# Weights in column halves and a new order of loads and engines in an attention and channel-mix kernel

## The chip, the cores and the metric

The kernel runs on one core of a Trainium2 chip. The metric is the device time in microseconds of one execution; the time before is the median of six runs.

## What is computed

```python
def _attn_ref(q, k, v):                      # q, k, v: 8 x 8 x 576 x 64, float32
    q_s = softmax of q over its last axis (64)
    k_s = softmax of k over the sequence (576)
    kv = np.einsum('bhsd,bhse->bhde', k_s, v)
    return np.einsum('bhsd,bhde->bhse', q_s, kv)

def _moe_ref(x, mu_k, mu_r, w_k, w_v, w_r):  # x: 8 x 576 x 512, heads side by side
    x_prev = x shifted by one row of the sequence, zero first
    xk = mu_k * x + (1.0 - mu_k) * x_prev
    xr = mu_r * x + (1.0 - mu_r) * x_prev
    k = np.maximum(xk @ w_k, 0.0)            # w_k: 512 x 1024
    v = k * k @ w_v                          # w_v: 1024 x 512
    r = 1.0 / (1.0 + np.exp(-(xr @ w_r)))    # w_r: 512 x 512
    return (r * v).astype(np.float32)
```

(The two softmaxes are written as words here.)

## The kernel before

Batches b are 0 to 7, and the eight heads of a batch are taken in two groups g of four. For each (b, g) the kernel loads q, k and v (line 308), takes exponentials on ACT (445), sums and scales the rows of q on DVE (458 to 466), transposes q on TensorE (498), sums kv (475), copies the transposed q (503), and multiplies it with kv (511). For batches 0 and 1 (ON_PE) the mix with mu is folded into the weights wp (555), so that TensorE writes the mixed xk and xr, which are evicted by ACT or DVE (568). For the others x is copied (605, 608), and DVE forms differences, scales and sums (617 to 627). xk and xr are rings of four batches in bfloat16.

The channel mix runs over units of 512 columns of that ring (the last of each half is 256). In a unit the eight products with columns of wk come first (712), each four matmuls over the 512 channels, then relu on ACT (697) and the square on DVE (701). Then for each 128 rows come the product with wr (745), its tanh (750), the product with wv in two halves of four matmuls (755), the gate on DVE (761) and the store (772). The first two units (early) take wk in two passes, four products on the first half of the channels, which group g = 0 makes, then on the second half. Four PSUM banks mm_a to mm_d serve all these products, and two double banks att_a and att_b serve the attention.

Weights are loaded by POOL's queue, which converts float32 to bfloat16: wk in two loads by channel pairs (wk0 for g = 0, wk1 for g = 1), wr in one, wv in two (wv0, wv1). The inputs of batch 0 are loaded by SP's and ACT's queues; those of batch 1 in halves by POOL, named by q, k or v, the batch, the group and a or b: q10a is the first half of q of batch 1, group 0. LOADS gives the order of POOL's queue up to the end of batch 1. The first load of POOL waits for the load first[GATE].

A planner in the kernel (class Plan) decides the order of every engine before anything runs. Each operation has an engine, an occupation, a latency, operations it waits for and buffers it takes and frees. set_due works backward: an operation is due ahead of what needs it by its latency, HOP and SPARE, and by its own early, which for the mixing operations is EARLY[2b + g] less EARLY_R when it makes xr. The products of the channel mix have due times from a running clock that starts at MAIN and grows by PACE times the product's time. order then plays the program through: the engine whose operation can start first takes it, and among operations that can start within LOOK of now the one due first. Loads take size/DMA_RATE each in one line, and a load of POOL counts as landed some time later. The emitted order is final: every engine runs its queue in order on the chip. ALONE says up to which (b, g) a pending product of q with kv is put in a block of its own, ahead of the next transposition, and after which it is joined with that. [...]

Of the kernel before, what the change touches and what calls it, by code (L numbers as in the profile page):

```python
# [18 lines left out]
LATE = 1e6  # L19
SPARE = 0.142  # L20
LOOK = {"PE": 0.017, "ACT": 0.686, "DVE": 0.274, "POOL": 0.03, "SP": 0.03}
EARLY = (-0.88, 2.53, 7.27, 7.81, 6.48, 1.05, 4.91, 4.86, 2.31, 3.67, 7.48, 5.23, -5.83,
         4.63, 1.92, 1.86)
EARLY_R = -0.92
MAIN = 17.0
PACE = 1.05
DMA_RATE = 404.0
# [6 lines left out]
ORDER = (0, 1, 2)  # L34
LOADS = ("wk0", "q10b", "wk1", "v10a", "q10a", "wr", "k10a", "wv0", "mu", "v10b", "k10b",
         "wv1", "k11b", "q11b", "q11a", "k11a", "v11a", "v11b")
GATE = 7
FILL = 0
FILL_AT = 1
FILL_END = 15.0  # L40
ON_PE = (0, 1)
CASTS = (("POOL", "POOL"), ("ACT", "DVE"), ("ACT", "ACT"))
QCOPY = ("ACT", "ACT", "DVE")
WIDE = "ACT"
ALONE = 8
EVAC = ((("ACT", "DVE"), ("ACT", "DVE")), (("DVE", "ACT"), ("ACT", "ACT")))
# [25 lines left out]
class Plan:  # L72
# [60 lines left out]
    def order(self):  # L133
# [15 lines left out]
        while left:  # L149
# [59 lines left out]
def kernel(  # L209
# [12 lines left out]
    nc = tc.nc  # L222
# [49 lines left out]
    def bank(slot):  # L272
        return ps[slot.pool][slot.index][:]
# [103 lines left out]
    rows_done = plan.add("PE", 0.86, 0.98, -501, emit_mu_rows, [rows_load, consts], [rows_slot])  # L377
    wide = plan.add(WIDE, 0.48 if WIDE == "ACT" else 0.6, 0.6 if WIDE == "ACT" else 0.7, 0, emit_mu_wide, [rows_done], [], [rows_slot])
    mu_split = [plan.add("POOL", 0.5, 0.6, -2 + m, lambda m=m: emit_mu_rest(m), [wide])
                for m in range(2)]  # L380

    def filler(slot):
        for _ in range(2):
            nc.tensor.matmul(bank(slot)[:, 0:128], lhsT=ident[:], rhs=ident[:], start=True,
                             stop=True)
# [23 lines left out]
    def emit_wv(h):  # L409
        n = FT // 2  # L410
        ap = bass.AP(tensor=moe_w_v.tensor, offset=moe_w_v.offset + h * n * C,
                     ap=[[FT * C, 128], [C, n], [1, C]])
        return nc.gpsimd.dma_start(out=wv_bf[:, h * n:(h + 1) * n, :], in_=ap)
# [262 lines left out]
    for _ in range(FILL):  # L676
        slot = Slot("mm")
        plan.add("PE", 0.12, 0.25, 2 * LATE, lambda slot=slot: filler(slot), [warmed[0]], [slot],
                 [slot])
# [5 lines left out]
    def unit(half, c0, n):  # L685
# [24 lines left out]
        def k_part(kf, fc, cts):  # L710
            for ct in cts:
                nc.tensor.matmul(bank(kf)[:, 0:n],  # L712
                                 lhsT=wk_bf[:, ct, fc::FT],
                                 rhs=xs[0][:, ct, c0:c0 + n],
                                 start=(ct == 0), stop=(ct == CT - 1))
# [134 lines left out]
```

## Time and profile before

| | |
|---|---|
| median of 6 runs | 203.84 us (202.52 to 204.48) |
| the profiled execution | 202.52 us |
| its span | 200.8 us |
| TensorE matmuls busy | 183.5 us (91%) |
| TensorE weight loads busy | 103.9 us (52%) |
| VectorE busy | 162.2 us (81%) |
| ScalarE busy | 137.3 us (68%) |
| GpSimd busy | 40.5 us (20%) |
| bytes moved | 40.72 MB, 203 GB/s on average |

Times within the profile are from the start of the span, which is shorter than the run's time by what lies around the program. Busy shares are averages over the span: which engine sets the time is read stage by stage, from the slices and from the chain that ended last. Moved bytes count a converting load by what it writes, half of what it reads.

### The profile page before, as it was taken

What the parts mean: (1) busy time and instruction counts of PE and PEld (TensorE: products, weight loads), DVE (VectorE), ACT (ScalarE), POOL (GpSimd) and SP (SyncE); (2) the same over time, 40 slices, a digit from 0 to 9 for tenths busy, and PEclk for the clock granted to TensorE, in tenths of its full rate; (3) what the DMA queues carried; (4) which work ended last, traced back from release to release, by engine and by line L of the source; (5) the groups of instructions that cost most, each with busy time, mean ns of one, the idle gap of its engine ahead of it and who ended that gap; (6) DMA issues with size and microseconds to landing.
All of it is one profiled execution on the core that took longest, in us unless ns stands there. A gap on an engine that the chain in (4) does not pass through costs nothing.

```text
span 200.8 us, 5308 instructions
## 1 busy us (share of the span) xinstructions
PE 183.5 (91%) x2146; PEld 103.9 (52%) x2171; DVE 162.2 (81%) x348; ACT 137.3 (68%) x212; POOL 40.5 (20%) x65
## 2 busy tenths in 40 slices
PE   2557899899999999999999999999999999999992
PEld 0234554446444654564476564456446554654761
DVE  2697755897999999999989999999999879732531
ACT  5583797699899789867499788945744652552440
POOL 1592447643153212501230000000000000000000
PEclk9999999999999999999999999999999999999999
DMA  6999999999999998994986130342026112402514
GB/s 191 388 247 276 239 288 405 389 401 412 386 401 402 405 370 256 295 363 141 320 264 208 31 76 3 69 96 49 3 54 136 24 44 64 105 0 52 118 42 105
DMA packets 15249, 40.72 MB, mean 203 GB/s; under 512 B 2285, under 2 KB 3065, under 8 KB 15225
## 3 DMA queue, kind: packets, MB, share of 16 engines
q0 software_dynamic: 7568, 27.40, 41.2%
q1 hardware_dynamic: 7208, 12.26, 21.0%
q10 hardware_dynamic: 448, 0.72, 1.2%
q8 instruction: 17, 0.28, 0.6%
q14 instruction: 8, 0.06, 0.1%
HBM read 33.56 MB, written 9.44 MB: 214 GB/s over the span
## 4 chain that ended last, share of the span: by engine, by line
PE 85%; DVE 6%; DMA 4%; issue 2%; ACT 1%; DVEq 0%; ACTq 0%
PE mm_b L755 10%; PE mm_d L712 9%; PE mm_c L712 8%; PE mm_c L755 7%; PE mm_d L755 7%; PE mm_a L755 7%; PE mm_b L712 7%; PE mm_a L712 5%; PE mm_c L745 4%; PE mm_a L745 4%; PE mm_d L745 3%; PE mm_b L745 3%; PE att_a L511 3%; PE att_b L511 3%; DMA raw_d<-in_q_dram 3%; PE att_b L498 2%
## 5 line engine op out<-in xcount | busy, mean ns | idle before, releaser
L712 PEld LDWEIGHTS <-wk_bf 128*128 128x128 bf16 x320 | 43.5, 144 | 20.8 <-issue 2.2
L712 PE MATMUL mm_d<-xk,wk_bf 128*128 128x512 bf16 (+1 forms) x94 | 23.9, 367 | 0.1
L755 PEld LDWEIGHTS <-k_b 128*128 128x128 bf16 x152 | 14.3, 98 | 15.3 <-issue 0.5
L745 PEld LDWEIGHTS <-xr 128*128 128x128 bf16 x144 | 13.9, 98 | 15.9 <-issue 0.2
L755 PEld LDWEIGHTS <-k_a 128*128 128x128 bf16 x144 | 13.4, 98 | 15.7 <-issue 0.9
L712 PE MATMUL mm_c<-xk,wk_bf 128*128 128x512 bf16 (+1 forms) x80 | 19.9, 357 | 0.6 <-issue 0.6
L712 PE MATMUL mm_b<-xk,wk_bf 128*128 128x512 bf16 (+1 forms) x75 | 18.9, 363 | 0.1
L712 PE MATMUL mm_a<-xk,wk_bf 128*128 128x512 bf16 (+1 forms) x62 | 15.3, 358 | 0.2
L755 PE MATMUL mm_b<-wv_bf,k_b 128*128 128x512 bf16 (+1 forms) x54 | 13.3, 363 | 0.2 <-issue 0.2
L745 PE MATMUL mm_c<-wr_bf,xr 128*128 128x512 bf16 x43 | 11.2, 379 | 0.1
L745 PE MATMUL mm_a<-wr_bf,xr 128*128 128x512 bf16 x39 | 10.2, 379 | 0.1
L755 PE MATMUL mm_c<-wv_bf,k_a 128*128 128x512 bf16 x39 | 10.1, 379 | 0.2 <-issue 0.2
L755 PE MATMUL mm_b<-wv_bf,k_a 128*128 128x512 bf16 x38 | 9.8, 379 | 0.2 <-issue 0.2
L755 PE MATMUL mm_a<-wv_bf,k_a 128*128 128x512 bf16 x30 | 8.1, 380 | 0.1
L755 PE MATMUL mm_d<-wv_bf,k_a 128*128 128x512 bf16 x32 | 8.2, 380 | 0.0
L755 PE MATMUL mm_d<-wv_bf,k_b 128*128 128x512 bf16 x32 | 8.2, 379 | 0.0
L745 PE MATMUL mm_d<-wr_bf,xr 128*128 128x512 bf16 x31 | 8.2, 379 | 0.1
L750 ACT ACTIVATE th_a<-mm_c 128x512 f32<-128x512 f32 x10 | 6.0, 603 | 3.1 <-PE mm_c L745 3.1
L755 PE MATMUL mm_a<-wv_bf,k_b 128*128 128x512 bf16 x29 | 7.6, 379 | 0.5 <-issue 0.5
L750 ACT ACTIVATE th_b<-mm_a 128x512 f32<-128x512 f32 x7 | 4.2, 604 | 4.5 <-PE mm_a L745 2.3
L755 PE MATMUL mm_c<-wv_bf,k_b 128*128 128x512 bf16 (+1 forms) x31 | 7.1, 352 | 0.2 <-issue 0.2
L745 PE MATMUL mm_b<-wr_bf,xr 128*128 128x512 bf16 x26 | 7.1, 379 | 0.1
(268 smaller groups left out, 415.4 us busy)
## 6 DMA issues: line engine op xcount, KB each, us to landing
out_dram<-ot_a SPq DMA_DIRECT2D x24, 128.0 KB, 4.2
out_dram<-ot_b SPq DMA_DIRECT2D x24, 128.0 KB, 3.4
out_dram<-ot_c SPq DMA_DIRECT2D x22, 128.0 KB, 2.4
raw_a<-in_q_dram POOLq DMA_DIRECT2D x3, 576.0 KB, 7.3
raw_c<-in_v_dram POOLq DMA_DIRECT2D x3, 576.0 KB, 8.0
raw_b<-in_k_dram POOLq DMA_DIRECT2D x2, 576.0 KB, 9.9
raw_d<-in_q_dram POOLq DMA_DIRECT2D x2, 576.0 KB, 10.6
raw_e<-in_k_dram POOLq DMA_DIRECT2D x2, 576.0 KB, 9.4
```

Source lines behind the costliest of these rows:

```text
L498: nc.tensor.transpose(out=transposed()[64 * u:64 * u + 64, hf, 64 * j:64 * j + 64], in_=qss[qs.index][r, j, 64 * u:64 * u + 64], identity= ...
L511: nc.tensor.matmul(bank(xp)[64 * hf:64 * hf + 64, u, at + c:at + e], lhsT=w[r, hf, :], rhs=qts[qt.index][r, hf, src:src + e - c], start=(n ...
L712: nc.tensor.matmul(bank(kf)[:, 0:n], lhsT=wk_bf[:, ct, fc::FT], rhs=xs[0][:, ct, c0:c0 + n], start=(ct == 0), stop=(ct == CT - 1))
L745: nc.tensor.matmul(bank(rps), lhsT=xs[1][:, ct, c:c + 128], rhs=wr_bf[:, ct // 2 + 2 * (ct % 2), :], start=(ct == 0), stop=(ct == CT - 1))
L750: nc.scalar.activation(out=ths[th.index][:], in_=bank(rps), func=ACT.Tanh, scale=0.5)
L755: nc.tensor.matmul(bank(vps)[:, 0:w], lhsT=k2s[k2.index][:, ft, 128 * m:128 * m + 128], rhs=wv_bf[:, ft, e:e + w], start=(ft == 0), stop=( ...
```

## The change

wk0, the part of wk for the first group's channels, is loaded in two column halves, wk0a and wk0b (columns 0 to 511 and 512 to 1023). The product fc used every eighth column from fc; it now uses every fourth column of one half, so that products 0 to 3 need wk0a and products 4 to 7 need wk0b. The rows of wv are loaded in the matching order. LOADS is another order: q10a comes first, then all of wk, and both parts of wv come later. The planner's constants SPARE, LOOK, EARLY, EARLY_R, MAIN, PACE, FILL_END and ALONE, its sizes of the weight loads and its allowance for a POOL load to land are others, so the order of all engines is another. The filler has another form, and the number of fillers stays 0; the choice of the engine for the wide copy of mu is written in another way, and stays ACT.

```diff
-SPARE = 0.142
-LOOK = {"PE": 0.017, "ACT": 0.686, "DVE": 0.274, "POOL": 0.03, "SP": 0.03}
-EARLY = (-0.88, 2.53, 7.27, 7.81, 6.48, 1.05, 4.91, 4.86, 2.31, 3.67, 7.48, 5.23, -5.83,
-         4.63, 1.92, 1.86)
-EARLY_R = -0.92
-MAIN = 17.0
-PACE = 1.05
+SPARE = 0.367
+LOOK = {"PE": 0.014, "ACT": 0.49, "DVE": 0.274, "POOL": 0.03, "SP": 0.03}
+EARLY = (-4.56, 2.11, 8.25, 13.06, 6.4, 0.7, -0.55, -0.78, 2.62, 0.78, 6.17, 8.08, -3.7,
+         4.17, 15.59, 5.15)
+EARLY_R = 3.13
+MAIN = 14.0
+PACE = 1.2
...
-LOADS = ("wk0", "q10b", "wk1", "v10a", "q10a", "wr", "k10a", "wv0", "mu", "v10b", "k10b",
-         "wv1", "k11b", "q11b", "q11a", "k11a", "v11a", "v11b")
+LOADS = ("q10a", "wk0a", "wk0b", "wk1", "k10a", "q10b", "wr", "mu", "v10b", "v10a", "k10b",
+         "wv0", "q11b", "wv1", "q11a", "k11b", "k11a", "v11a", "v11b")
...
-FILL_END = 15.0
+FILL_END = 14.0
...
-ALONE = 8
+ALONE = 6
...
                 if op.engine == "POOL":
-                    op.end += 1.4 if op.size > 1000 else 0.6
+                    op.end += 1.0 if op.size > 600 else 0.8
...
-    def emit_wk(g):
-        ap = bass.AP(tensor=moe_w_k.tensor, offset=moe_w_k.offset + g * 128 * F,
-                     ap=[[F, 128], [256 * F, 2], [1, F]])
-        return nc.gpsimd.dma_start(out=wk_bf[:, 2 * g:2 * g + 2, :], in_=ap)
+    def emit_wk(g, c, e):
+        ap = bass.AP(tensor=moe_w_k.tensor, offset=moe_w_k.offset + g * 128 * F + c,
+                     ap=[[F, 128], [256 * F, 2], [1, e - c]])
+        return nc.gpsimd.dma_start(out=wk_bf[:, 2 * g:2 * g + 2, c:e], in_=ap)
...
-    wk_done, wv_done = [], []
-    for g in range(2):
-        wk_done.append(plan.add("POOL", 0.8, 0.8, LOADS.index(f"wk{g}"), lambda g=g: emit_wk(g), gate,
-                                size=1140.0))
-    wr_done = plan.add("POOL", 0.8, 0.8, LOADS.index("wr"), emit_wr, gate, size=1140.0)
+    wk_done, wv_done = {}, []
+    for name in LOADS:
+        if name.startswith("wk"):
+            g = int(name[2])
+            c, e = {"": (0, F), "a": (0, F // 2), "b": (F // 2, F)}[name[3:]]
+            o = plan.add("POOL", 0.8, 0.8, LOADS.index(name),
+                         lambda g=g, c=c, e=e: emit_wk(g, c, e), gate, size=1250.0 * (e - c) / F)
+            for h in range(2):
+                if c <= h * F // 2 < e:
+                    wk_done[g, h] = o
+    wr_done = plan.add("POOL", 0.8, 0.8, LOADS.index("wr"), emit_wr, gate, size=1200.0)
...
     def emit_wv(h):
         n = FT // 2
-        ap = bass.AP(tensor=moe_w_v.tensor, offset=moe_w_v.offset + h * n * C,
-                     ap=[[FT * C, 128], [C, n], [1, C]])
+        ap = bass.AP(tensor=moe_w_v.tensor, offset=moe_w_v.offset + h * n * 128 * C,
+                     ap=[[n * C, 128], [C, n], [1, C]])
         return nc.gpsimd.dma_start(out=wv_bf[:, h * n:(h + 1) * n, :], in_=ap)
 
     for h in range(2):
         wv_done.append(plan.add("POOL", 0.8, 0.8, LOADS.index(f"wv{h}"), lambda h=h: emit_wv(h), gate,
-                                size=1140.0))
+                                size=1200.0))
...
                 nc.tensor.matmul(bank(kf)[:, 0:n],
-                                 lhsT=wk_bf[:, ct, fc::FT],
+                                 lhsT=wk_bf[:, ct, F // 2 * (fc // 4) + fc % 4:F // 2 * (fc // 4 + 1):4],
                                  rhs=xs[0][:, ct, c0:c0 + n],
                                  start=(ct == 0), stop=(ct == CT - 1))
...
-                        + [wk_done[h] for h in gs] + [mms_[i]],
+                        + [wk_done[h, fc // 4] for h in gs] + [mms_[i]],
```

More of the change, by code (lines that the diff above doesn't have):

```diff
@@ L377 @@
     rows_done = plan.add("PE", 0.86, 0.98, -501, emit_mu_rows, [rows_load, consts], [rows_slot])
-    wide = plan.add(WIDE, 0.48 if WIDE == "ACT" else 0.6, 0.6 if WIDE == "ACT" else 0.7, 0, emit_mu_wide, [rows_done], [], [rows_slot])
+    wide = plan.add(WIDE, *{"ACT": (0.48, 0.6), "DVE": (0.6, 0.7), "POOL": (0.75, 0.85)}[WIDE], 0,
+                    emit_mu_wide, [rows_done], [], [rows_slot])
     mu_split = [plan.add("POOL", 0.5, 0.6, -2 + m, lambda m=m: emit_mu_rest(m), [wide])
@@ L382, in filler @@
     def filler(slot):
-        for _ in range(2):
-            nc.tensor.matmul(bank(slot)[:, 0:128], lhsT=ident[:], rhs=ident[:], start=True,
-                             stop=True)
+        nc.tensor.matmul(bank(slot)[:, 0:256], lhsT=ident[:],
+                         rhs=ident[:, None, :].to_broadcast((128, 2, 128)), start=True, stop=True)
     gate = [first[GATE]]
     sync = mybir.DependencyInfo(mybir.DependencyClass.Sync, mybir.DependencyReason.DATA)
-    def emit_wk(g):
-        ap = bass.AP(tensor=moe_w_k.tensor, offset=moe_w_k.offset + g * 128 * F,
-                     ap=[[F, 128], [256 * F, 2], [1, F]])
-        return nc.gpsimd.dma_start(out=wk_bf[:, 2 * g:2 * g + 2, :], in_=ap)
+    def emit_wk(g, c, e):
+        ap = bass.AP(tensor=moe_w_k.tensor, offset=moe_w_k.offset + g * 128 * F + c,
+                     ap=[[F, 128], [256 * F, 2], [1, e - c]])
+        return nc.gpsimd.dma_start(out=wk_bf[:, 2 * g:2 * g + 2, c:e], in_=ap)
     def emit_wr():
@@ L677 @@
         slot = Slot("mm")
-        plan.add("PE", 0.12, 0.25, 2 * LATE, lambda slot=slot: filler(slot), [warmed[0]], [slot],
+        plan.add("PE", 0.108, 0.25, 2 * LATE, lambda slot=slot: filler(slot), [warmed[0]], [slot],
                  [slot])
```

## The prediction

> **What bounds the kernel now.** I read the page first, its slices, then the idle time of TensorE by stage, then the chain of waits up to 45 us, then the POOL timeline and the landing times of the weight loads.
>
> ```profile
> PE   2557899899999999999999999999999999999992
> DVE  2697755897999999999989999999999879732531
> DMA  6999999999999998994986130342026112402514
> GB/s 191 388 247 276 239 288 405 389 401 412 386 401 402 405 370 256 295 363 141 320 264 208 31 76 3 69 96 49 3 54 136 24 44 64 105 0 52 118 42 105
> ```
>
> A slice is 5.02 us. From the fifth slice on TensorE is nearly full, and VectorE with it up to about 150 us. The DMA engines are full from 5 to about 75 us. So the order of loads can only decide what comes early; it can't shorten the sum of the loads.
>
> The busy time by stage (columns: stretch, its length, then busy time of PE, PEld, DVE, ACT, POOL with counts, clock, DMA share, GB/s) shows how little is left:
>
> ```profile
> 17.60:20.00 2.40, 2.34 (x7) 0.97 (x6) 1.97 (x5) 0.37 (x1) 0.21 (x1) 1.00 1.08 316
> 20.00:22.00 2.00, 1.38 (x31) 0.85 (x30) 0.77 (x2) 1.06 (x2) 1.46 (x3) 1.00 1.19 193
> ...
> 37.00:40.00 3.00, 2.27 (x90) 1.27 (x88) 3.00 (x8) 1.20 (x4) 1.12 (x3) 1.00 1.03 388
> ```
>
> Length less PE busy, summed over all stretches from 17.6 to 196.4 us, is 3.7 us: 0.62 in 20 to 22, 0.73 in 37 to 40, 2.1 spread over everything after 43. A schedule can win those 3.7, and what lies ahead of the first large matmul. The chain (start, length, what) says how that begins:
>
> ```profile
> 11.35 1.34 DVE qs_b L466 x2
> 12.74 0.69 PE att_b L498 x29
> ...
> 15.42 0.65 ACT xk L568
> 16.11 0.69 PE att_b L511 x8
> 16.80 0.48 PE att_a L511 x10
> 17.28 0.37 issue
> 17.66 0.63 PE mm_c L712
> 18.29 0.85 PE mm_d L712 x2
> ...
> 20.69 0.77 DVE xr L568
> 21.50 0.44 PE att_b L511 x8
> 21.94 0.58 PE mm_c L712 x2
> ...
> 38.62 0.65 ACT xr L568
> 39.30 0.48 PE att_b L498 x36
> ```
>
> The reader is to see three things. The first product with wk starts at 17.66. TensorE then stands for two evictions of xr (20.69 and 38.62), which sit in its queue ahead of work that could run. And the first wk matmuls take about 0.42 us apart instead of 0.216, five of them, some 1.0 us: TensorE is not up to speed after its small attention work (the granted clock reads 1.00 all the same).
>
> **The loads, step by step.** POOL's timeline (start, length of the issue, what it waited for):
>
> ```profile
> 14.44 0.58 POOL L413 DMA_DIRECT2D wv_bf<-in_moe_w_v_dram  x1
> 16.11 0.54 POOL L324 DMA_DIRECT2D mu_sb<-in_moe_mu_k_dram  x1 [1.10 <-DMA wk_bf<-in_moe_w_k_dram]
> ...
> 19.79 0.57 POOL L308 DMA_DIRECT2D raw_g<-in_v_dram  x1 [2.45 <-DMA wk_bf<-in_moe_w_k_dram]
> ```
>
> From the landing times of the loads (issue time from the timeline plus "DMA to landing"): wk0 9.91 + 5.9 = 15.8, wk1 11.36 + 8.1 = 19.5, wr 13.16 + 10.2 = 23.4, wv0 14.44 + 13.1 = 27.5, wv1 21.21 + 10.1 = 31.3. Between wk0 and wv1 lie 15.5 us, four weights and six half inputs. A half input is 0.295 MB, at the 405 GB/s of the slices 0.73 us, six 4.4 us; so a weight of 1 MB in float32 costs (15.5 - 4.4)/4 = 2.8 us.
>
> The new order is q10a, wk0a, wk0b, wk1, k10a, q10b, wr, mu, v10b, v10a, k10b, wv0, q11b, wv1, and so on. With these prices: wk0a lands at 15.8 - 1.4 + 0.7 = 15.1, wk0b at 16.5, wk1 at 19.5 (the same bytes lie ahead of it), k10a 20.2, q10b 20.9, wr 23.4 (again the same bytes), k10b, the last of batch 1's first half, at 25.6 (three half inputs after wr) where it was 27.5 + 1.5 = 29.0, wv0 at 28.4 (was 27.5), wv1 at 31.9 (was 31.3). The last inputs of batch 1 end where they did. So batch 1's first pair of head groups comes 3.4 us earlier, wv0 0.9 later, wv1 0.6 later.
>
> What each is worth. Before, wk0 at 15.8 was just in time: TensorE waited until 16.1 for the eviction of xk, not for wk0. wk0a at 15.1 alone therefore gives nothing; it gives at most what the planner, seeing it earlier, brings forward of the chain to xk. That chain had slack in it: the weights wp_a of the first group are made at 13.5 from kv sums that ended at 9.9, because VectorE did the second group in between. If the first group goes first, wk matmuls could start between 15.2 (wk0a) and 17.66. They are followed by a wait for wk1 at 19.5 in any case, and there is room for mixing blocks in between. I take 0.8 us here; ends 0 and 2.0.
>
> The wait at 20 to 22: wk1 is there at 19.5, and the second half of the first four products starts only at 21.94, behind mixing of xr. EARLY_R goes from -0.92 to 3.13, which makes the mixing of xr due 4.05 us later than before against that of xk: r is first used at 27.8, so TensorE can take wk1's products first. I take 0.4 of the 0.62; ends -0.4 (a new wait of the same kind) and 0.6.
>
> The wait at 37 to 40: it is batch 1's second group, held by VectorE, whose row sums for that group (eq_a, made by 34.2) began only at 36.26. VectorE stood still for 3.08 us until 32.02, waiting for the first group's kv. With the first group in 3.4 us earlier, that hole is filled with its copies and weights, and the second group's sums can start by 34.3. I take 0.6 of the 0.73; ends 0 and 0.73. The same head start may shorten the VectorE-held stretch at 113 to 122 us (0.45 us of TensorE idle in 115 to 125); I take 0 for it.
>
> wv0: first use at 30.22 against landing 27.5, and the second half of wv at 34.09 against 31.3. If all ahead moves up by 1.8, the first product with wv is reached at 28.4, which is where wv0 now lands. The cover is gone but for attention blocks of batch 1, which are now ready by then (transposition and kv 0.7, mixing 0.37 each). I take a loss of 0.2; ends 0 and 0.9.
>
> Splitting wk0. It adds one issue on POOL: between 0.54 and 0.89 us by the DMA rows, beside a DMA queue that is backed up. POOL runs eight issues without a break from 9.91 to 15.02 and then waits for its first load to land (mu_sb at 16.11 for wk0, raw_g, the eleventh, at 19.79 for the third): there are eight in flight. With nine names ahead that window moves on by one; wv0, now thirteenth, waits for k10a at 20.2, wv1, fifteenth, for wr at 23.4. Both have over 3 us of queued bytes ahead of them then, so no bubble. [...] Segments are 2 KB of source in place of 4 KB; no row shows that. Ends 0 and 2.0; I take 0.1, hidden.
>
> wk's column step. Rows of F are permuted so that a weight tile is read with a step of four elements, not eight.
>
> ```profile
> L712 PEld LDWEIGHTS <-wk_bf 128*128 128x128 bf16 x320 | 43.5, 144 | 20.8 <-issue 2.2
> L745 PEld LDWEIGHTS <-xr 128*128 128x128 bf16 x144 | 13.9, 98 | 15.9 <-issue 0.2
> ```
>
> The strided load takes 144 ns, the packed one 98. [...] The trace says what it is worth: four products of 512 columns take 0.86 us, of 256 columns 0.44, also under loads of 144 ns. They lie beneath the matmuls. What shows is the first load of a burst after a wait or a change of tiling: 2.2 us of idle "issue" in nine cases, 9 x 46 ns = 0.4 at most. I take 0.1; ends 0 and 0.4.
>
> ALONE from 8 to 6 lets two more mixing blocks run together with the next transposition: at 0.1 to 0.2 us of switch each (0.16 "issue" at 122.82), 0.2 us gained, unless a joined block waits for the inputs of the next (then as much lost). wv's row order keeps its 8 KB pieces: nothing. The filler's new form isn't used (FILL is 0). SPARE, LOOK, EARLY, MAIN, PACE change the order of every engine after 43 us; there 2.1 us of idle can be won, and more than that lost. I take 0.
>
> Sum: -0.8 - 0.4 - 0.6 + 0.2 - 0.1 - 0.2 = -1.9 us. The profiled execution took 202.52 us, its span 200.80; so 198.9 span and 200.6 for a run like it. It is the lowest of six, 1.32 under the median; taken off the median, 203.84 - 1.9 = 201.9.
>
> **The rivals.** *The start is set by wk1 and batch 1 anyway* (no change). wk1 and wr land as before, and so does the last input of batch 1. If TensorE only waits at other places, it is 203.2 to 204.4. For it: full DMA up to 75 us. Against: the three waits named stood for evictions, not for loads.
>
> *Late evictions in the middle (slower).* The new EARLY values bring batch 1's second group 5.25 us and batch 7's first 13.7 us forward, and batch 3 5.5 us back. VectorE is busy 4.6 to 5.0 of each 5 us from 60 to 125 us. Where attention work is put ahead of relu squares and gates there, the four mm banks come free late and TensorE stands. At 113 to 121 the chain already lies on VectorE for about 7 us. The stall at 38.6 shows the price of one such place, 0.73 us; five of them in the six batches that follow are 3.7 us, less the 1.9 of the forecast: +1.8, 205.6. It decides as soon as over 1.9 us of new idle time appears after 43 us, about three places. Against: VectorE's total work is unchanged. For: batch 3's products follow each other with no spare, and batch 3's mixing now comes later.
>
> *More gain.* All of the start (2.0), both waits (1.35) and half of the later idle: -4.3, 199.5. It needs loads never to bind.
>
> **How the numbers follow.** The measurement can tell about 0.5% (1.0 us). Forecast, 200.6 to 202.8: 0.37; more gain: 0.12; no change: 0.18; slower: 0.33 (from 204.9 up). The range takes the low end of the gain and most of the slow case: 199.2 to 206.4. Faster 0.49, same 0.18, slower 0.33.
>
> **What would show it.** The first wk matmul near 16.9; wk products on the second half of xk right after 19.5; no xr eviction in the chain around 20 and 38; first wv product at 28.5 with little wait; LDWEIGHTS of wk near 98 ns with the spacing of matmuls unchanged; idle time of TensorE from 43 us to the last matmuls at about 2.1 us. If wk0a lands after 16, or TensorE's idle time after 43 us is over 3.5 us, the forecast is wrong.

## The result and the profile after

The changed kernel takes 202.64 us (median of 35 runs, 201.18 to 204.64), the kernel before 203.67 (72 runs, 202.52 to 204.68). The ratio is 0.9939 with an interval of 0.9923 to 0.9954: faster by 0.6%, 1.2 us at this size. This ratio leaves out the seven runs of the changed kernel that lie more than 1.5% above its fastest, as slow runs; with them its mean is 0.8 us under that of before. Forecast were 201.9 us and a gain of 1.9.

The two profiles do not show this difference as it stands. The profiled execution of before took 202.52 us, its fastest; that of the changed kernel 203.59, 0.95 above its median. Its span is 201.8 us where before has 200.8. So the two traces are good for seeing what moved, and bad for a sum of the times. The slices of the page after:

```profile
PE   3356999999999999999999999999999999999992
DVE  2597378798999999999969999999998998432531
DMA  6999999999999999993892130242033204402514
GB/s 198 375 250 223 300 256 369 390 402 405 390 398 407 405 377 280 385 374 142 245 361 76 31 74 3 52 99 62 3 84 77 52 3 104 104 0 52 116 43 104
```

TensorE reads 6 in the fourth slice (15 to 20 us) where it read 7, and the DMA engines are as full as before. The stages that the prediction looked at (stretch, length, then busy time of PE, PEld, DVE, ACT, POOL with counts, clock, DMA share, GB/s):

```profile
17.60:20.00 2.40, 1.25 (x3) 0.33 (x4) 1.64 (x5) 0.64 (x1) 0.56 (x1) 1.00 1.09 271
20.00:22.00 2.00, 2.00 (x23) 1.03 (x23) 0.76 (x1) 0.62 (x1) 0.46 (x1) 1.00 1.14 269
...
37.00:40.00 3.00, 2.95 (x15) 1.27 (x13) 2.22 (x4) 3.00 (x6) 1.64 (x3) 1.00 1.03 390
```

PE busy is the second number of each row, after the length. Both waits that stood in before, 0.62 us in 20 to 22 and 0.73 in 37 to 40, are gone. A new one stands in 17.6 to 20, where TensorE works 1.25 of 2.40 us. The chain of waits (start, length, what) names it:

```profile
11.66 7.05 DMA wk_bf<-in_moe_w_k_dram
18.71 0.05 issue
18.75 0.61 PE mm_c L718
19.37 0.85 PE mm_d L718 x2
...
38.54 0.86 PE mm_d L761 x4
39.40 0.86 PE mm_b L751 x4
40.26 0.37 PE att_a L517 x8
40.63 0.31 PE att_b L504 x36
```

The reader is to see two things. Before stood at 38.6 ahead of the transposition of batch 1's second group; here products with wv (L761) and wr (L751) and a mixing block lie in the same place, and the transposition (L504) follows at 40.63 without a wait (its first record starts at 40.46; a chain leaves out what overlaps). And the first product with wk is now held by a load of wk: wk0b, issued at 11.66, landed at 18.7.

Four milestones place the difference in each profiled execution, before and in the experiments below: the span, the first record of a wk product, the start of the first product with wr (all wk products of the first unit are then done), and what of the span lies behind that. A star marks a trace that lacks the record of the very first wk matmul; the time at which its weights load stands in brackets.

| kernel | span | first wk product | first wr product | span behind it |
|---|---|---|---|---|
| before | 200.8 | 17.66* (17.21) | 27.63 | 173.1 |
| before_wk0_split | 200.8 | 17.71 | 27.71 | 173.1 |
| changed | 201.8 | 18.75* (17.52) | 29.39 | 172.4 |
| after_again | 201.8 | 18.58 | 29.74 | 172.1 |
| after_wk0_whole | 200.0 | 17.98 | 27.89 | 172.1 |
| after_wk0_apart | 200.5 | 18.01 | 27.42 | 173.1 |
| after_wk0_channels | 200.7 | 17.65 | 28.34 | 172.4 |
| after_whole_step8 | 200.2 | 17.46 | 28.15 | 172.1 |
| after_whole_gate6 | 200.4 | 17.87 | 28.48 | 171.9 |
| after_loads_of_before | 207.1 | 24.80* (24.38) | 35.01 | 172.1 |
| before_loads_of_after | 207.4 | 19.25* (18.81) | 34.29 | 173.1 |

In before's order of engines 173.1 us lie behind the first wr product, in the changed order about 172.1 in most rows (172.4 in two, 173.1 in after_wk0_apart, which is taken up below). So the gain lies behind the start, and the start loses in both profiled executions of the changed kernel: its first wr product comes 1.8 and 2.1 us later than in before.

### The profile page after: what moved, and what is told of

Read it like the earlier page. It is cut to its first block, busy times and chain, and to the rows that moved or that the text cites. A ratio compares the mean times of both kernels' runs of the same rounds, so it can differ in the third digit from the quotient of the medians.

```text
span 201.8 us, 5314 instructions
## 1 busy us (share of the span) xinstructions
PE 184.6 (91%) x2147; PEld 96.8 (48%) x2171; DVE 160.8 (80%) x348; ACT 136.7 (68%) x212; POOL 40.9 (20%) x66
## 4 chain that ended last, share of the span: by engine, by line
PE 83%; DMA 11%; DVE 1%; issue 1%; POOL 1%; SPq 0%; ACT 0%; DVEq 0%
PE mm_c L761 9%; PE mm_a L718 9%; PE mm_d L718 9%; PE mm_d L761 7%; PE mm_a L761 7%; PE mm_c L718 6%; PE mm_b L761 6%; PE mm_b L718 6%; PE mm_b L751 5%; PE mm_d L751 4%; DMA wk_bf<-in_moe_w_k_dram 3%; DMA out_dram<-ot_a 3%; PE mm_c L751 3%; DMA raw_d<-in_q_dram 3%; PE mm_a L751 3%; PE att_b L517 2%
## 5 line engine op out<-in xcount | busy, mean ns | idle before, releaser
L718 PEld LDWEIGHTS <-wk_bf 128*128 128x128 bf16 x320 | 35.4, 114 | 28.9 <-issue 2.4
L718 PE MATMUL mm_a<-xk,wk_bf 128*128 128x512 bf16 (+1 forms) x96 | 24.3, 362 | 0.3 <-issue 0.2
L761 PEld LDWEIGHTS <-k_b 128*128 128x128 bf16 x152 | 14.5, 98 | 15.7 <-issue 0.7
L751 PEld LDWEIGHTS <-xr 128*128 128x128 bf16 x144 | 13.9, 98 | 15.9
L761 PEld LDWEIGHTS <-k_a 128*128 128x128 bf16 x144 | 13.4, 98 | 15.5 <-issue 0.4
L718 PE MATMUL mm_c<-xk,wk_bf 128*128 128x512 bf16 (+1 forms) x66 | 16.0, 358 | 1.2 <-DMA wk_bf<-in_moe_w_k_dram 1.2
L751 PE MATMUL mm_b<-wr_bf,xr 128*128 128x512 bf16 x50 | 13.2, 379 | 0.1
L761 PE MATMUL mm_c<-wv_bf,k_a 128*128 128x512 bf16 x46 | 12.1, 379 | 0.2 <-issue 0.2
L761 PE MATMUL mm_c<-wv_bf,k_b 128*128 128x512 bf16 x47 | 12.1, 379 | 0.2 <-issue 0.2
L756 ACT ACTIVATE th_a<-mm_b 128x512 f32<-128x512 f32 x12 | 7.1, 595 | 6.4 <-PE mm_b L751 4.9
L761 PE MATMUL mm_d<-wv_bf,k_b 128*128 128x512 bf16 x39 | 10.1, 379 | 0.2 <-issue 0.2
L761 PE MATMUL mm_b<-wv_bf,k_a 128*128 128x512 bf16 x38 | 10.0, 379 | 0.2 <-issue 0.2
L761 PE MATMUL mm_a<-wv_bf,k_b 128*128 128x512 bf16 (+1 forms) x39 | 9.4, 358 | 0.1
L751 PE MATMUL mm_d<-wr_bf,xr 128*128 128x512 bf16 x34 | 9.1, 379 | 0.1
L761 PE MATMUL mm_d<-wv_bf,k_a 128*128 128x512 bf16 x28 | 7.5, 379 | 0.4 <-issue 0.3
L707 DVE TENSOR_TENSOR k_a<-rel_b 128x512 bf16<-128x512 bf16 (+1 forms) x14 | 5.6, 397 | 2.8 <-ACT rel_b L703 2.8
L707 DVE TENSOR_TENSOR k_a<-rel_c 128x512 bf16<-128x512 bf16 (+1 forms) x13 | 5.1, 389 | 3.4 <-ACT rel_c L703 3.4
L751 PE MATMUL mm_c<-wr_bf,xr 128*128 128x512 bf16 x28 | 7.2, 379 | 0.1
L751 PE MATMUL mm_a<-wr_bf,xr 128*128 128x512 bf16 x28 | 7.2, 379 | 0.0
```

What stands on the lines that cost most here:

```text
L707: nc.vector.tensor_tensor(out=k2s[k2.index][:, fc, 0:n], in0=rels[rel.index][:, 0:n], in1=rels[rel.index][:, 0:n], op=ALU.mult)
L718: nc.tensor.matmul(bank(kf)[:, 0:n], lhsT=wk_bf[:, ct, F // 2 * (fc // 4) + fc % 4:F // 2 * (fc // 4 + 1):4], rhs=xs[0][:, ct, c0:c0 + n], ...
L751: nc.tensor.matmul(bank(rps), lhsT=xs[1][:, ct, c:c + 128], rhs=wr_bf[:, ct // 2 + 2 * (ct % 2), :], start=(ct == 0), stop=(ct == CT - 1))
L756: nc.scalar.activation(out=ths[th.index][:], in_=bank(rps), func=ACT.Tanh, scale=0.5)
L761: nc.tensor.matmul(bank(vps)[:, 0:w], lhsT=k2s[k2.index][:, ft, 128 * m:128 * m + 128], rhs=wv_bf[:, ft, e:e + w], start=(ft == 0), stop=( ...
```

## Experiments

Every kernel ran beside the kernel before on the same chip (medians of before 203.59 to 203.73); ratios are to that. Names that begin with "after" keep the changed kernel's order of engines, those with "before" the old one; the planner was not run anew for any, only what it emits was edited. Theories at the outset: the engines' order took the wait at 38 away (O in some of the quoted texts), or the earlier loads did; the split of wk0 brings the first products forward, does nothing, or costs; and TensorE's slow start sets the beginning (C).

**The changed kernel once more** (no edit).

> The changed kernel once more, beside the others and for a second profile. Ratio to the kernel before 0.992 to 0.995 as measured. Theory A (a false wait): the first product on the second channel of wk0 starts only when the second column half wk0b has landed, so it again starts within 0.2 us of wk0b's landing (18.7 in the first profile), not of wk0a's (15.4). Theory B (the split releases the products early): it starts near 17.5, and the 1.2 us of waiting in the first profile was an accident of that execution.

203.40 us (201.28 to 204.66, 12 runs), ratio 0.9976 (0.9945 to 1.0007); by itself it can't be told from before. The kernel spreads over 3.4 us. This profile repeats the other: the first wr product late (29.74), the wait at 38 gone, 172.1 us behind.

**Order of the engines against order of the loads.** Two kernels with one half of the change each: the changed engines with POOL's 18 loads in before's sequence, and the reverse. In both, wk0 is one load.

```diff
+    turn = ("wk0", "q10b", "wk1", "v10a", "q10a", "wr", "k10a", "wv0", "mu", "v10b", "k10b",
+            "wv1", "k11b", "q11b", "q11a", "k11a", "v11a", "v11b")
+    done = plan.order()
...
+    for n, name in zip(spots, turn):      # spots: POOL's places of these loads in done
+        done[n] = byname[name]
```

> The changed kernel's order on TensorE, VectorE, ScalarE and SyncE, wk0 in one load, but POOL's 18 loads up to the end of batch 1 in the sequence of the kernel before. Theory O (the gain is in the order of the engines; TensorE's work from 35 to 42 us is arranged so that the wait for the eviction at 38.6 has other work ahead of it): no new wait there, the time stays within 0.5 us of 202.33, the one with wk0 whole. Theory L (the prediction's: the gain comes from batch 1's first group landing earlier): the stall of about 1.1 us is back, 203.3 or more.

> The reverse: the order of the engines of the kernel before, wk0 in one load, and the loads in the changed sequence. Theory O: the stall at 38.6 stays, wk0 lands about 0.7 us later and the first wk product up to 0.5 us later: ratio 1.000 to 1.004. Theory L: the stall of 0.7 to 1.1 us goes: ratio 0.996 or less.

208.22 us, ratio 1.0222 (1.0186 to 1.0259), and 207.92 us, ratio 1.019 (1.0154 to 1.0226). They are 4.5 and 4.2 us slower than before. Why is seen in the rows (start, length, engine, line, what, idle before and its releaser) of after_loads_of_before, ACT's first, TensorE's last:

```profile
22.02 0.68 ACT L451 ACTIVATE eq_c<-raw_g 128x576 bf16<-128x576 f32 x1 [6.23 <-DMA raw_g<-in_q_dram]
22.61 0.62 ACT L574 CAST xk<-att_b 128x576 bf16<-128x576 f32 x1
```

```profile
23.28 0.69 PE L517 MATMUL att_b<-qt_b,wp_c 64*64 64x288 bf16 x8 [6.70 <-ACT xk L574]
```

The changed order puts the exponentials of q10a ahead of the eviction of xk on ACT, because its own loads bring q10a first; with the old loads q10a is late, ACT stands 6.23 us for it, and the eviction comes behind, at 22.61. In before_loads_of_after ACT stands 6.18 us for another half of q. These two orders only work as a pair.

The two kernels also bear on the wait at 38, which lies 5 to 7 us later in them. The two halves (the stretch of after_loads_of_before, then the transposition of before_loads_of_after):

```profile
43.00:46.00 3.00, 3.00 (x22) 1.27 (x24) 2.60 (x5) 3.00 (x7) 1.44 (x2) 1.00 1.03 392
```

```profile
45.96 0.48 PE L498 MATMUL att_b<-ident,qs_b 64*64 64x64 bf16 x36 [0.74 <-ACT xr L568]
```

With the changed engines TensorE is full although the loads are the old ones; with the old engines the same 0.74 us is there although the loads are the new ones. Everything behind the start is some 6 us late in both, so the loads of batch 1 are early for either order. That makes the second half the stronger one: 173.1 us lie behind its first wr product as in before, though its k10b (the last input of batch 1's first group) landed at 27.6, as early as in the changed kernel. The wait went with the engines' order.

What the wait was for, the rows name only in part. These are VectorE's and ScalarE's rows of before, then TensorE's (the kv product of the first group, the transposition of the second); then VectorE's and TensorE's of the changed kernel:

```profile
32.02 0.76 DVE L503 COPY qt_c<-att_b 128x1152 bf16<-128x1152 bf16 x1 [3.08 <-PE att_b L475]
36.26 1.41 DVE L458 TENSOR_REDUCE rsum_d<-eq_a 128x9 f32<-128x576 bf16 x2
37.83 1.41 DVE L466 TENSOR_TENSOR qs_b<-eq_a,rrec_d 128x576 bf16<-128x576 bf16 x2
38.62 0.64 ACT L568 CAST xr<-att_a 128x576 bf16<-128x576 f32 x1 [1.12 <-PE att_a L511]
31.48 0.47 PE L475 MATMUL att_b<-vv_a,ek_a 64*64 64x65 bf16 x36
39.30 0.48 PE L498 MATMUL att_b<-ident,qs_b 64*64 64x64 bf16 x36 [0.73 <-ACT xr L568]
```

```profile
31.54 0.74 DVE L509 COPY qt_c<-att_b 128x1152 bf16<-128x1152 bf16 x1
33.90 0.74 DVE L464 TENSOR_REDUCE rsum_d<-eq_a 128x9 f32<-128x576 bf16 x1
39.35 0.76 DVE L472 TENSOR_TENSOR qs_b<-eq_a,rrec_d 128x576 bf16<-128x576 bf16 x1
30.66 0.47 PE L481 MATMUL att_b<-vv_a,ek_a 64*64 64x65 bf16 x36
40.46 0.48 PE L504 MATMUL att_b<-ident,qs_b 64*64 64x64 bf16 x36
```

The row of before puts its wait down to the eviction of xr, which ended at 39.26. But VectorE's scaled q (qs_b), which is what the transposition reads, was ready only at 39.24, and the eviction reads att_a, while the transposition writes att_b. So without the eviction TensorE would have stood as long, to within 0.02 us: VectorE held it. VectorE was late because it had stood 3.08 us for the first group's kv product, which TensorE does at 31.48, 3.9 us behind its first wr product. In the changed order that product comes 1.3 us behind it; VectorE doesn't stand, starts the second group's sums at 33.90 and has qs_b ready at 40.11, ahead of the transposition.

**wk0 in one load.**

```diff
-                         lambda g=g, c=c, e=e: emit_wk(g, c, e), gate, size=1250.0 * (e - c) / F)
+                         lambda g=g, c=c, e=e: emit_wk(g, 0, F) if c == 0 else None, gate, ...)
```

> The changed kernel with every engine's order kept, but wk0 loaded in one transfer where wk0a stood. Theory A: the split only costs (segments of 1 KB written, 105 to 129 ns each, against 178 for 2 KB; about 1 us for wk0 and all behind it), so wk0 lands at 17.3 to 17.7, wk1 about 1 us earlier than 21.3, TensorE waits under 0.3 us for wk0, and the time is 0.5 to 1.2 us under the changed kernel (201.5 to 202.1). Theory B: the split brings the gain, so this one is 0.5 us or more above it (203.1 and more).

202.33 us (200.43 to 203.03, 11 runs), ratio 0.9909 (0.9877 to 0.9942), on the chip on which after_again gave 0.9976 (0.9945 to 1.0007). The intervals part by 0.0003. The split doesn't bring the gain; without it the kernel is no slower and probably faster.

**The two halves in tiles of their own**, so that a product can only wait for its half.

```diff
-    wk_bf = const.tile([128, CT, F], BF16, name="wk_bf")
+    wk_bf = [const.tile([128, 2, F // 2], BF16, name=f"wk_{x}") for x in "ab"]
+    wk_bf.append(const.tile([128, 2, F], BF16, name="wk_c"))
```

> The changed kernel with every engine's order kept and wk0 still loaded in two halves, but each half and wk1 in a buffer of its own, so that a product waits only for the half that it reads. Theory A: the first four products on wk0 start at 17.5 without a wait, some 1.2 us earlier than in the first profile; wk1 lands late as before (about 21.3), so of the 1.2 us about half shows at the end: 201.8 to 202.4. Theory B: nothing changes (202.4 to 202.9).

202.08 us (201.67 to 202.39, 6 runs), ratio 0.9918 (0.9887 to 0.9948). What the tiles change is seen in TensorE's weight loads of the changed kernel, then in the products of after_again, then in those of after_wk0_apart:

```profile
17.52 0.11 PEld L718 LDWEIGHTS <-wk_bf 128*128 128x128 bf16 x1 [0.20 <-issue]
18.75 0.15 PEld L718 LDWEIGHTS <-wk_bf 128*128 128x128 bf16 x2 [1.11 <-DMA wk_bf<-in_moe_w_k_dram]
```

```profile
18.58 0.62 PE L718 MATMUL mm_c<-xk,wk_bf 128*128 128x512 bf16 x1
19.65 0.62 PE L718 MATMUL mm_c<-xk,wk_bf 128*128 128x512 bf16 x1 [0.45 <-DMA wk_bf<-in_moe_w_k_dram]
```

```profile
18.01 1.04 PE L720 MATMUL mm_c<-xk,wk_a 128*128 128x512 bf16 x2
```

In the changed kernel the weights of the first channel tile load at 17.52, those of the second stop until 18.75. wk0a had landed at 15.4, wk0b lands at 18.7: the second load of weights, which reads only columns of wk0a, waits for wk0b. After_again does the same at 19.65, when its wk0b lands. With own tiles two matmuls follow each other at 18.01, although wk_b lands only at 18.8. So in the changed kernel the products do not need only their half: the wait is false. What makes it is not shown; the strided read of the second channel tile lies within the extent of wk0b's write, that of the first does not.

This kernel has the earliest first wr product of those without fillers (27.42) and still 173.1 us behind it. There a load binds instead. POOL's row of the changed kernel that issues k10b, and TensorE's row of after_wk0_apart that k10b holds:

```profile
21.54 0.54 POOL L308 DMA_DIRECT2D raw_h<-in_k_dram  x1 [1.99 <-DMA wk_bf<-in_moe_w_k_dram]
```

```profile
29.67 0.47 PE L482 MATMUL att_b<-vv_a,ek_a 64*64 64x65 bf16 x34 [0.51 <-ACT ek_a L452]
```

k10b is the twelfth load of POOL and is issued when wk1, the fourth, has landed: eight in flight, as in before (the trace shows POOL's loads to use eight semaphores in turn). In after_wk0_apart it is issued at the same time, 21.59, but lands at 28.9 instead of 27.7; why is not shown. Its exponentials follow, and TensorE waits at batch 1's first group: laid beside after_again, matmul by matmul, it falls back by 0.98 us at this product, and by less than 0.1 in all the rest. So this one wait is the whole of the 1.0 us by which 173.1 exceeds 172.1. The changed order of engines needs k10b early; landing as late as in before, it costs as much as the order gains.

**What the split costs in transfer.** Two kernels: before with wk0 in two loads and the permuted rows, and the changed kernel with wk0 split by channels (each half [F,128],[1,F], as long a piece as the whole load has).

> The kernel before with its order of all engines, but wk0 loaded in two halves one behind the other and the rows of F permuted as in the change. Theory A: all loads behind wk0 land about 0.8 to 1 us later; the first products with wk start at most 1 us later, the first with wv has 2.7 us to spare, so the time is 0 to 1 us longer (ratio 1.000 to 1.005). Theory B: ratio 0.997 or less.

> The changed kernel with wk0 still in two transfers at the same places, but divided by channels in place of columns: each half is 128 contiguous rows of 1024, written in 2 KB pieces. Theory S (the cost of the split lies in the 1 KB pieces): wk0's second half lands within 0.5 us of where wk0 whole did (17.3 to 19.0), pieces take about 178 ns, wk1 lands at 20.0 or earlier relative to a POOL start at 10.2, and the time is that of wk0 whole, 201.9 to 202.5. Theory N (the cost is the further transfer as such): wk1 at 21.3, the time that of the changed kernel, 202.6 to 203.4.

203.47 us, ratio 0.9987 (0.9968 to 1.0007), and 202.50 us, ratio 0.9928 (0.99 to 0.9956). In before's order the split is worth nothing in either direction. In the changed order the last part of wk0 lands after the start of POOL's first load by 8.5 us (changed), 8.3 (after_again), 8.1 (after_wk0_apart), against 6.6 in one load and 7.3 split by channels. The stretch from 14 to 16 us of the changed kernel, then of after_wk0_whole:

```profile
14.00:16.00 2.00, 1.69 (x49) 1.16 (x41) 2.00 (x9) 1.76 (x3) 2.00 (x5) 1.00 0.79 106
```

```profile
14.00:16.00 2.00, 2.00 (x70) 1.49 (x63) 1.94 (x11) 1.94 (x3) 2.00 (x4) 1.00 1.11 187
```

The DMA engines move 106 GB/s at a share of 0.79 instead of 187 at 1.11. The column halves are written in pieces of 1 KB, twice as many as of 2 KB. In the mean over the packets of the stretch in which wk0 lands, one takes 113 ns on a DMA engine (changed kernel, 13.0 to 18.8), a piece of 2 KB 189 (after_wk0_whole, 13.0 to 17.3): a fifth more time for these bytes. But more pieces don't explain engines that stand idle. In the fifth us behind POOL's start the three traces with column halves in the changed order have DMA shares of 0.60, 0.77 and 0.56, after_wk0_whole 1.11, and the two kernels split by channels 1.04 and 0.84 (after_combined). before_wk0_split has the same pieces and no dip there (190 GB/s in 14 to 16), only an earlier one (0.60 in 11.4 to 12.4, where before has 0.99), and its wk1 lands only 0.2 us later after POOL's first load than before's. So the column halves seem to have a part in it, and what makes the dip stays open.

**The column step.** wk0 whole, and the permutation of rows undone:

```diff
-                                 lhsT=wk_bf[:, ct, F // 2 * (fc // 4) + fc % 4:F // 2 * (fc // 4 + 1):4],
+                                 lhsT=wk_bf[:, ct, fc::FT],
```

> wk0 in one load, the changed kernel's order, and the row permutation undone: weights of wk are read with a step of eight elements again, wv's rows as before. Loads beneath matmuls: the weight loads take 143 ns in place of about 110, the matmul spacing is unchanged, the time within 0.3 us of 202.33. If the weight loads bound the matmuls: 0.5 us or more above it.

202.61 us (201.79 to 205.14, 12 runs), ratio 0.9955 (0.9928 to 0.9983), against 0.9909 with step 4; the intervals overlap. The groups (line, out<-in, count, busy and mean ns of one, idle before), of the changed kernel, then of after_whole_step8:

```profile
L718 PEld LDWEIGHTS <-wk_bf 128*128 128x128 bf16 x320 | 35.4, 114 | 28.9 <-issue 2.4
```

```profile
L718 PEld LDWEIGHTS <-wk_bf 128*128 128x128 bf16 x320 | 43.4, 144 | 20.5 <-issue 2.1
```

With step four there are eight us of weight loading less, and the time behind the first wr product is the same 172.1 (after_wk0_whole against after_whole_step8). The loads lie beneath the matmuls.

**TensorE's slow start.** Twelve matmuls that write an unused part of a bank: nine ahead of the second group's transposition, three ahead of its mixing; once in after_wk0_whole, once in before.

```diff
+                nc.tensor.matmul(ps["mm"][3][:, 256:512], lhsT=ident[:],
+                                 rhs=ident[:, None, :].to_broadcast((128, 2, 128)), start=True,
+                                 stop=True)
```

> The changed kernel's order with wk0 in one load, and twelve filler matmuls of 256 columns put on TensorE in its idle stretches ahead of the first wk products (nine before the second group's transposition, three before its mixing); their results are not used. Theory C (the start is slow and differs from run to run because TensorE is not up to speed, products at 0.42 us apart instead of 0.216 until 19 to 25 us, depending on the execution): the wk products are 0.216 apart from the first one, the time falls by 1 to 2 us to 200.3 to 201.3, and the spread of the runs shrinks to under 1.2 us. Theory D (the slow spacing is that of the loads or of the weight reads): nothing changes, 202.0 to 202.6, spread as before.

> The kernel before with the same twelve fillers at the same two places. Theory C: faster by 0.8 to 1.3 us, ratio 0.993 to 0.996, spread under 1.2 us in place of 2. Theory D: ratio 0.999 to 1.003.

202.11 us (200.42 to 202.78, 8 runs), ratio 0.9919 (0.9889 to 0.9949), and 203.58 us, ratio 1.0005 (0.998 to 1.0029). To see what the fillers do, first the start of the changed kernel:

```profile
21.25 1.04 PE L718 MATMUL mm_a<-xk,wk_bf 128*128 128x512 bf16 x2
22.09 1.06 PE L718 MATMUL mm_b<-xk,wk_bf 128*128 128x512 bf16 x2
23.08 0.69 PE L517 MATMUL att_b<-qt_b,wp_d 64*64 64x288 bf16 x8
23.56 0.69 PE L517 MATMUL att_a<-qt_b,wp_d 64*64 64x288 bf16 x12
24.19 0.62 PE L718 MATMUL mm_c<-xk,wk_bf 128*128 128x512 bf16 x2
```

Two matmuls of 512 columns take 1.04 us at 21.25 and 0.62 at 24.19; mixing blocks of 0.69 take 0.44 later on. TensorE is at half pace until 24.2, through the first eight wk matmuls (two for each of four products) and four mixing blocks. In before it is quick from 19.4. With fillers (after_whole_filled):

```profile
19.12 0.38 PE L718 MATMUL mm_c<-xk,wk_bf 128*128 128x512 bf16 x1 [1.16 <-DMA wk_bf<-in_moe_w_k_dram]
19.33 0.59 PE L718 MATMUL mm_d<-xk,wk_bf 128*128 128x512 bf16 x2
```

The matmuls are 0.21 us apart from the first on, even behind a wait of 1.16 us. So the fillers cure the pace, and the time doesn't follow. In after_whole_filled the wait for wk0 takes the place; the first wr product is 0.6 us earlier than in after_wk0_whole (27.29 against 27.89), and 0.8 us more lie behind it (172.9). The trace of before_filled shows where such time goes:

```profile
102.68 0.25 PE L475 MATMUL att_a<-vv_b,ek_b 64*64 64x65 bf16 x5 [0.95 <-issue]
```

A pause of 0.95 us in the middle of a group (31 matmuls before it, 5 after), for which no wait is shown. after_whole_filled has one of 0.32 us at 76.72, ahead of the fourth matmul of a product with wr. Laid beside the unfilled kernels matmul by matmul, TensorE loses 1.09 us (before_filled) and 0.48 us (after_whole_filled) at these two places, and at most 0.2 elsewhere. What makes the pauses was not found.

**The gate of POOL's first load** (after_wk0_whole, waiting for first[6] instead of first[7]):

```diff
-            tc.add_manual_dep(op.made.ins, gate.pop().made.ins.name, sync)
+            gate.pop()
+            tc.add_manual_dep(op.made.ins, first[6].made.ins.name, sync)
```

> wk0 in one load, the changed kernel's order, and POOL's first load waits for the first half of the second group's q of batch 0 in place of the second. If the landing of wk0 sets the start in part of the executions, the loads start 0.4 to 1.1 us earlier, wk0 lands at 17.0 or earlier, and the time falls to 201.5 to 202.0 with a smaller spread. If the inputs of batch 0, which then share the DMA engines, set it, the time is 202.3 to 203.3.

202.28 us (201.33 to 203.31, 8 runs), ratio 0.9923 (0.9891 to 0.9955): the same. POOL's first load starts at 10.8 us, without the edit at 10.7, so the gate is not what holds it, and the run says nothing on an earlier start.

**A combination**: split by channels, k10b ahead of the two loads of mu, and the fillers.

> What the runs point to, put together on the changed kernel's order: wk0 in two transfers divided by channels (2 KB pieces; the products wait for what they read), the last input of batch 1's first group issued ahead of the mu loads, which then no longer wait in front of it, and the twelve fillers. If start, loads and clock are what is left to win: first wk product at 17.5 without a wait and 0.216 apart, 0.8 to 1.5 us under wk0 whole (200.8 to 201.5) with a spread under 1.5 us. If the spread comes from elsewhere (b0's inputs, other stalls): 201.8 to 202.4.

202.65 us (201.54 to 203.29, 12 runs), ratio 0.994 (0.9919 to 0.9961). It doesn't beat the single edits. k10b landed at 28.0, the first wr product came at 27.24, the earliest of all, and 173.8 us lie behind. One pause of it, at the same matmul as in after_whole_filled, with all four of its group recorded:

```profile
77.79 0.38 PE L756 MATMUL mm_a<-wr_bf,xr 128*128 128x512 bf16 x1 [0.49 <-issue]
```

The lowest medians are after_wk0_apart (202.08), after_whole_filled (202.11), after_whole_gate6 (202.28) and after_wk0_whole (202.33). All lie under the changed kernel's 202.64, but their intervals overlap with its own: none is shown to be faster than it, save after_wk0_whole against the run on its own chip.

## Why the prediction was right, and where its steps were not

The sign and the size came out (1.2 where 1.9 was forecast, inside the range). Two terms won, both behind the start: the wait at 37 to 40, with half of its cause right, and fewer changes of tiling, about 0.5 where 0.2 was taken; a new wait of 0.40 took some of it back. The largest term, the start, failed, and what the lost wait at 20 to 22 gave went into it. That the sum came near is in part luck.

**The wait at 37 to 40, taken at 0.6: right size, the holder right, its cause half right.** The wait of 0.73 us is gone. The prediction held that VectorE makes it, standing for the first group's kv and so starting the second group's sums only at 36.26, and that these could start by 34.3. They started at 33.9, and the hole of 3.08 us is gone. (Its other reading, that TensorE stands at 38.62 for an eviction of xr, is what the row says and not what held it.) What the prediction had wrong is why the first group comes sooner: it took a landing 3.4 us earlier, at 25.6. k10b landed at 27.7, only 1.3 us earlier than before, and the second group's inputs, but for one half of q, landed 0.2 to 2.4 us later. TensorE's order puts the first group's kv ahead of products that stood in front of it, and with the old order and the new loads the wait stays. The landing counts in another way: where k10b came at 28.9 (after_wk0_apart), the new order lost at the first group what it gained at the second.

**The rest behind the start.** In two traces without missing records the stretch from the first wr product to the last product is 168.5 us long (before_wk0_split, 27.71 to 196.19) and 167.5 (after_again, 29.74 to 197.25). Idle time of TensorE fell from 0.87 us (0.74 of the wait above, 0.13 at 121.8) to 0.40, in one new place; so some 0.5 must be matmul time. TensorE changes between 64-row and 128-row tiling 44 times there instead of 48, which makes 0.12 us for each if all of it lies there (an estimate), inside the 0.1 to 0.2 that the prediction took; its 0.16 at 122.82 stands in front of a group "x3", so that row shows no switch. That is the term of ALONE (taken at 0.2) with the other reordering; it was not tried by itself.

**The idle time behind 43 us, "2.1 us": a misreading.** The stretch from 43 to 196.4 us in before, before_wk0_split and after_again:

```profile
43.00:196.40 153.40, 151.32 (x1656) 86.46 (x1670) 131.94 (x274) 107.21 (x166) 18.09 (x25) 1.00 0.54 175
```

```profile
43.00:196.40 153.40, 153.27 (x1677) 79.54 (x1670) 132.15 (x274) 107.18 (x166) 18.06 (x25) 1.00 0.54 177
```

```profile
43.00:196.40 153.40, 153.00 (x1672) 79.18 (x1671) 131.63 (x277) 108.72 (x167) 18.47 (x26) 1.00 0.54 180
```

With the same order, before_wk0_split has 21 matmul records more than before and 0.13 us idle instead of 2.08. The idle time was missing records: a group "x3" with 0.16 us of "issue" in front is a group of four that lost its first. The changed order has 0.40 us, in one place:

```profile
106.73 0.41 PE L517 MATMUL att_a<-qt_a,w_c 64*64 64x512 bf16 x4 [0.40 <-ACT xb_a L614]
```

The prediction's 17.66 for the first wk product is a missing record too: the weights of that product's first matmul load at 17.21. So a schedule could win not 3.7 but some 1.5 us and the start, and the later idle time that the rival *more gain* counted on (its parts add up to 4.4, not 4.3) was never there. The slower rival, late evictions in the middle, needed 1.9 us of new idle time and got 0.4.

**The start, taken at -0.8, and the wait at 20 to 22, at -0.4: the step that failed.** The wait of 0.62 is gone, as forecast. But the start didn't get shorter, for three reasons.

The chain to xk did not move. The prediction saw slack in it and wk products from 16.9 on. In every kernel with the changed order and loads but the filled ones TensorE still stands 0.73 us for xk, and mixing resumes behind that at 16.4 in the changed kernel, against 16.1 and 16.6 in before and before_wk0_split. The changed kernel's first wk weights load at 17.5, and its products on wk1 begin at 24.2, not right after 19.5 (wk1 landed at 21.3).

The false wait for wk0b. Against before_wk0_split, whose records are complete, the second matmul with wk comes at 18.75 instead of 18.13 (17.71 and one spacing of 0.42): +0.62.

The pace. From there to the first wr product are 10.64 us instead of 9.58, +1.06, for the same wk matmuls and four mixing blocks; with the 0.62 of the lost wait that is 1.68 more. Four wk matmuls more go at 0.42 instead of 0.216 (0.8), and the four mixing blocks take 2.2 us instead of 1.4 (0.8). All told the first wr product is 0.62 + 1.06 = 1.68 later, 29.39 against 27.71. The prediction had seen the five slow matmuls in before and priced no change in them.

The clock row of the profile reads 1.00 in all these stretches, so it doesn't show the pace. Counted from the end of the wait for xk, the quick pace comes after 2.8 us in before_wk0_split (16.6 to 19.4), 3.3 in before, 3.4 in after_wk0_apart (16.9 to 20.3), 4.5 in after_wk0_whole, 6.0 in after_whole_step8 and in after_whole_gate6, 6.1 in after_wk0_channels, 6.4 in after_again and 7.8 in the changed kernel (16.4 to 24.2). What sets this time is not shown. The changed kernel has the false wait of 1.16 us in it and is quick 5.4 us behind its end (18.75); before_loads_of_after, with waits of 1.47, 0.94 and 1.28 us, is slow until 30.4, 4.4 us behind the last of them. That doesn't show that waits hold the pace down, and the false wait isn't needed for a slow start: after_whole_step8, after_whole_gate6 and after_wk0_channels wait for no wk0 and go at half pace through the same eight wk matmuls. Against after_whole_gate6 the changed kernel loses 1.3 us from the end of the wait for xk to the first wr product, 0.8 by the wait and 0.5 by the pace. With one trace for each kernel, what of the pace belongs to the kernel and what to the execution isn't shown. Nor is it shown that the pace makes the wide spread of the changed kernel: after_whole_filled, quick from the first product, spreads over 2.4 us as well.

At the medians the start must be about even. The run takes 1.8 us more than the span; 202.64 less 1.8 and less 172.1 to 172.4 puts the first wr product at 28.4 to 28.7, and for before 203.67 less 1.8 and 173.1 at 28.8. This is an estimate, since both profiled executions of the changed kernel lie about 1 us above its median. By it the gain is the 1.0 behind the start and little else.

**The split, taken at 0.1 and hidden: mis-sized.** wk0a landed at 15.4 (15.1 forecast), wk0b at 18.7 (16.5), wk1 at 21.3 (19.5), wr at 25.2 (23.4). POOL began 0.3 us later; of the rest, the last part of wk0 is 1.9 us later than in one load, counted from the first load (1.7 and 1.5 in after_again and after_wk0_apart). But before_wk0_split lost hardly anything (its wk1 landed 0.2 us later after POOL's first load than before's), so this doesn't hold in general. No run shows the 0.1, or the upper end of 2.0, as what a split costs: the runs showed 1.5 to 1.9 us in the changed order and 0.2 in before's.

**wv late, taken at +0.2: nothing.** wv0 landed at 29.7 and wv1 at 32.9, but the first product with wv stood only at 32.9, not at 28.5, and needs no more than wv0.

**Weight loads, taken at -0.1: nothing.** No run shows the 98 ns that were forecast for a step of four: it takes 114, and 98 is the packed load's. The spacing of matmuls (0.216 us) did not move, as said.

## What to carry to other kernels

A strip of idle time worth winning must be seen in a trace whose matmul counts are complete; short "issue" gaps ahead of incomplete groups were no time at all here (2.08 us in before, 0.13 in before_wk0_split with 21 records more). When a load is split so that work can start on a part, give the parts their own buffers, and look in the profile which load released the first user (here the wrong half, 1.16 us of waiting). When a wait is put down to one engine, look whether another input of the same instruction came just as late (here at 39.24 against 39.26). Order of engines and order of loads are one plan: taking one without the other cost 4.2 to 4.5 us here, more than three times what the pair gained.

## What the runs showed of the hardware that was not expected

- The pace of TensorE at the start makes 1.7 us between two profiled executions with the same matmuls (changed kernel, before_wk0_split), while the clock row reads 1.00; 0.42 us per 512 columns against 0.216.
- Weight loads with a column step of eight, four and one element of bfloat16 take 144, 114 and 98 ns.
- A load split in column halves landed its last part 1.5 to 1.9 us later in one order of loads; the same split in the other order cost wk1 0.2 us. Not explained.
- In the three kernels with twelve matmuls more in the beginning, TensorE pauses 0.32 to 0.95 us on "issue" inside a group of matmuls, in two of them at the same matmul. Not explained.
